# Attention loads in pairs of tokens and pairs of chunks, with a block swap on GpSimd and a new order of the output turn

## The chip, the cores and the metric

The kernel runs on one core of a Trainium2 chip. A core has five engines with their own instruction queues: TensorE (PE; its weight loads are listed as PEld), VectorE (DVE), ScalarE (ACT), GpSimd (POOL) and SyncE (SP). SP only issues DMAs here. Engines meet through semaphores, and each engine works its queue strictly in order. The metric is the device time of one execution in microseconds (us), lower is better.

## The reference

The program is causal windowed attention, then two mixtures of experts. Only the attention is touched by the change. Cut to what matters:

```
q, k, v: [4 batch, 8 heads, 576 tokens, 64]
scores = q @ k.T / 8 ; bias = -slope[h] * |i - j| ; kept where 0 <= i - j < 128
attn   = softmax(scores + bias)            # rows
x      = (attn @ v) -> [2304 tokens, 512]  # heads side by side
x      = soft MoE(x; phi, w1, w2)          # 8 experts, 4 slots each
out    = Sinkhorn-gated MoE(x; w_gate, m1, m2)
```

The array x is 2304 by 512, all inputs are float32, and the two expert stages read 33.5 MB of weights each.

## The kernel before

**Tiles and steps.** Two batch items go together (j = 0, 1), so there are two pairs of items, each with nine chunks of 64 query tokens: 18 tiles t. A step s is one tile and one half of the heads: t = s // 2, half hf = s % 2, so there are 36 steps. A half has four heads, in two head pairs g. A chunk sees its own and the two chunks before it: 192 keys.

**One step.** `emit_qk` (L169) makes scores in PSUM on TensorE. `emit_sm` (L188) adds the bias and takes the row extreme on VectorE, four operations at L203. `emit_exp` (L209) takes exponentials on ScalarE. One step later `emit_nm` (L216) scales the rows on VectorE by the reciprocal sums: L219, L220 and four operations at L222, which read and write SBUF alone. Two steps later `emit_pt` (L224) turns the weights on TensorE and ScalarE copies them out of PSUM (L234). Three steps later `emit_pv` (L237) multiplies by the values. After the second half of a tile, VectorE copies the outputs to `xT` (L271). `emit_x` (L273), called by `turned` (L464), turns them on TensorE and ScalarE copies them to `xn` (L278). After every fourth tile, `group` (L343) adds the logits of the first mixture (L284) and its running sums, in slices of one a step.

**Queries and keys.** `load_nat` (L127) loads one chunk of k and one of q, token per partition: 64 partitions for each batch item, eight heads of 64 numbers each, so a DRAM run is 256 bytes. `emit_tr` (L147) turns them on TensorE, and VectorE copies them to `kT`, a ring of four chunks, and to `qT`. For ring places that must be readable past the ring's end, ScalarE makes a second copy (L158). Keys are turned for the next tile in the first half's step, queries two head pairs a step, right after the scores.

**Orders and pools.** The order of the work is the order in which the step loop (L475 to L526) calls these functions: it fixes every engine's queue. PSUM has three banks for turns (`ps_t`, tag "pt", used in rotation by every turn and by the logits) and three for scores (`ps_s`). SP's queue carries all loads in program order: k and q, v (`load_v`), and the weights of the expert stages, prefetched one part a step by `load_part` (L57) from the list `pre` (L455).

**Heads of the second item.** The score multiply puts head a of item j into partitions by `a ^ j` (L182), so the second item's rows would come out with two heads exchanged: the bias table `rel_sb` has a second version for it (L440, L450), and `emit_pv` undoes it (L262).

Of the kernel before, what the change touches and what calls it, by code (L numbers as in the profile page):

```python
# [20 lines left out]
NPRE = 8  # L21
# [3 lines left out]
def tile_kernel(ctx: ExitStack, tc: tile.TileContext, q, k, v, phi, w1, w2, w_gate, m1, m2, rel, out):  # L25
# [69 lines left out]
    with tc.manual_schedule():  # L95
        with ExitStack() as ab:
# [5 lines left out]
            with ExitStack() as at:  # L102
                nat = at.enter_context(tc.tile_pool(name="nat", bufs=2))
# [14 lines left out]

                rel_sb = one.tile([128, 2, 4, 192], F32, name="rel_sb")


                qT = one.tile([128, 4, 2, 64], F32, name="qT")
# [4 lines left out]
                def load_nat(t):  # L127
                    bp, c = divmod(t, NCH)
                    for nm, src in (("k", k), ("q", q)):
                        nt_ = nat.tile([128, H, D], F32, tag=nm + "n", name=nm + "n")  # L130
                        for j in range(2):
                            nc.sync.dma_start(
                                out=nt_[CH * j:CH * j + CH],
                                in_=src[2 * bp + j, :, CH * c:CH * c + CH, :].rearrange("h i d -> i h d"))
                        natt[nm, t] = nt_
# [11 lines left out]
                def emit_tr(t, nm, gs=range(4)):  # L147
                    src = natt[nm, t]
                    ps = ps_t.tile([128, 4, 128], F32, tag="pt", name="pt")
                    for i, g in enumerate(gs):  # L150
                        nc.tensor.transpose(
                            ps[:, i, :], src[:, 2 * g:2 * g + 2, :].rearrange("p a d -> p (a d)"), idn)
                    pv_ = ps[:, 0:len(gs), :].rearrange("p g (j i) -> p g j i", j=2)
                    if nm == "k":
                        sl_ = t % 4
                        nc.vector.tensor_copy(out=kT[:, :, :, CH * sl_:CH * sl_ + CH], in_=pv_)
                        if sl_ < 2 and t >= 4:
                            nc.scalar.copy(out=kT[:, :, :, CH * (sl_ + 4):CH * (sl_ + 5)], in_=pv_)  # L158
                    else:
                        nc.vector.tensor_copy(out=qT[:, gs[0]:gs[-1] + 1], in_=pv_)  # L160
# [8 lines left out]
                def emit_qk(s):  # L169
# [3 lines left out]
                    k0 = CH * ((t - nch + 1) % 4)  # L173
# [4 lines left out]
                    for gg in range(2):  # L178
                        g = 2 * hf + gg
                        for j in range(2):  # L180
                            for a in range(2):
                                r0, c0 = CH * (a ^ j), CH * a  # L182
                                nc.tensor.matmul(ps[j][c0:c0 + CH, gg, col:192], lhsT=qT[r0:r0 + CH, g, j, :],
# [4 lines left out]
                def emit_sm(s):  # L188
# [8 lines left out]
                    for hh in range(4):  # L197
# [7 lines left out]
                            in1=rel_sb[:, j, 2 * hf + gg, col:192], scale=-0.125, scalar=3e38,  # L205
# [31 lines left out]
                def emit_pv(s):  # L237
# [18 lines left out]
                    for i0 in range(0, len(steps), 2):  # L256
                        for gg in range(2):
                            g = 2 * hf + gg
                            for i in (i0, i0 + 1):
                                j, vc, r0, r1, blk = steps[i]  # L260
                                for a in range(2):
                                    o = 128 * blk + 64 * (a ^ j)  # L262
# [116 lines left out]
                def group_end():  # L379
# [17 lines left out]
                    mm = sc_[:, 0, 0:NS]  # L397
# [10 lines left out]
                    selx = sc_[:, 0, NS:2 * NS]  # L408
                    selc = sc_[:, 0, 2 * NS:3 * NS]
# [6 lines left out]
                    rcs = sc_[:, 0, 3 * NS:4 * NS]  # L416
# [20 lines left out]
                load_nat(0)  # L437
                nc.sync.dma_start(out=rel_sb[:, 0, 3, :], in_=rel)
                for j in range(2):
                    nc.sync.dma_start(out=rel_sb[CH * j:CH * j + CH, 1, 3, :], in_=rel[CH * (1 - j):CH * (2 - j), :])  # L440
                load_nat(1)
# [3 lines left out]
                emit_tr(0, "k")  # L445
                warm(None, ps, idn, 3)
                for g in range(4):
                    eng = nc.scalar.mul if g < 2 else nc.gpsimd.tensor_scalar_mul
                    for j in range(2):
                        eng(rel_sb[:, j, g, :], rel_sb[:, j, 3, :], -(2.0 ** (2 - 2 * g)))  # L450
                emit_tr(0, "q", range(0, 2))
                emit_tr(0, "q", range(2, 4))

                NST = 2 * NT
# [791 lines left out]
```

## Time and profile before

| | us |
|---|---|
| median of 3 runs | 967.4 (966.14 to 967.91) |
| the profiled execution, its own time | 964.41 |
| span of the profile (first to last instruction) | 962.6 |
| TensorE busy in the span | 925.3 (96%) |
| VectorE busy | 739.3 (77%) |
| ScalarE busy | 611.4 (64%) |
| GpSimd busy | 542.1 (56%) |

The shares are averages over stages with different limits. The attention is the first 16% or so of the span; after that the expert stages keep TensorE nearly always busy. The attention's step loop runs from 8.0 us (first bias operation of step 0) to 142.1 us (first bias operation of step 35). A row of the profile that ends in brackets says how long the engine was idle just before it, and who ended the wait.

### The profile page before, as it was taken

How to read it: one execution, taken by the hardware profiler on the slowest of the kernel's cores; microseconds unless marked ns; L12 is line 12 of the kernel's file. 1: busy time of each engine (PE TensorE's matmuls, PEld its weight loads, DVE VectorE, ACT ScalarE, POOL GpSimd, SP SyncE). 2: the span in 40 equal slices, each digit the busy share in tenths (PEclk: the TensorE clock that was granted, in tenths of full speed). 3: DMA queues.
4: the chain of work that ended last, by engine and by line, in shares of the span. 5: the costliest groups of instructions: out<-in, count | busy, mean ns of one | idle time of the engine just before them, and what ended most of it. 6: DMA issues, size and time to landing. Idle time of an engine off the chain costs nothing.

```text
span 962.6 us, 24531 instructions
## 1 busy us (share of the span) xinstructions
PE 925.3 (96%) x9629; PEld 781.5 (81%) x9629; DVE 739.3 (77%) x1920; ACT 611.4 (64%) x1493; POOL 542.1 (56%) x624
## 2 busy tenths in 40 slices
PE   7898889889999999999999999999999999999997
PEld 5666665357888888888888888888888888888886
DVE  6988896666888777787778777877777778777775
ACT  5877784746777777666656664766576656764442
POOL 1000001214688579848974986589658956985442
PEclk9999999999999999999999999999999999999999
DMA  8999998960200400140023002200220020001222
GB/s 184 251 254 233 265 296 291 379 232 2 99 2 2 153 35 2 25 164 1 2 79 109 1 1 90 99 1 2 94 94 1 2 97 4 1 2 34 56 47 64
DMA packets 94659, 90.20 MB, mean 94 GB/s; under 512 B 63696, under 2 KB 67792, under 8 KB 94544
## 3 DMA queue, kind: packets, MB, share of 16 engines
q1 hardware_dynamic: 94544, 88.64, 32.1%
q8 instruction: 75, 1.23, 0.5%
q14 instruction: 40, 0.33, 0.1%
HBM read 82.07 MB, written 4.72 MB: 90 GB/s over the span
## 4 chain that ended last, share of the span: by engine, by line
PE 74%; DVE 2%; ACT 1%; issue 0%; DVEq 0%
PE x L1051 38%; PE y L1051 28%; PE z L979 6%; PE m L681 1%; DVE ops L992 0%; DVE s L1004 0%; PE m L556 0%; DVE acc L1063 0%; DVE prob L948 0%; ACT acc L1061 0%; ACT ops L989 0%; DVE rs L936 0%; ACT r L1000 0%; PE m L942 0%; ACT t L564 0%
## 5 line engine op out<-in xcount | busy, mean ns | idle before, releaser
L1051 PEld LDWEIGHTS <-ops 128*128 128x128 f16 x6048 | 591.9, 98 | 75.5 <-issue 4.9
L1011 POOL TENSOR_TENSOR ops<-s,ops 128x512 f16<-128x512 f32 x287 | 332.0, 1159 | 224.2 <-ACT ops L1008 218.2
L1051 PE MATMUL x<-w2h,ops 128*128 128x256 f16 x2304 | 414.3, 273 | 3.9 <-ACT acc L1061 2.7
L1051 PE MATMUL y<-w2h,ops 128*128 128x256 f16 x1728 | 318.3, 273 | 0.1
L1051 PE MATMUL x<-w2l,ops 128*128 128x256 f16 x1152 | 314.2, 273 | 0.0
L1008 ACT CAST ops<-s 128x512 f16<-128x512 f32 x288 | 177.6, 617 | 212.6 <-DVE s L1004 210.2
L1051 PE MATMUL y<-w2l,ops 128*128 128x256 f16 x864 | 235.1, 273 | 0.0
L1065 DVE SCALAR_TENSOR_TENSOR acc<-x,pe,acc 128x256 f32<-128x256 f32 x252 | 121.7, 483 | 77.3 <-PE x L1051 75.8
L989 ACT ACTIVATE ops<-z 128x512 f16<-128x512 f32 x216 | 128.4, 594 | 36.0 <-PE z L979 33.1
L992 DVE SCALAR_TENSOR_TENSOR ops<-z,ops 128x512 f16<-128x512 f32 x216 | 146.9, 680 | 0.0
L1065 DVE SCALAR_TENSOR_TENSOR acc<-y,pe,acc 128x256 f32<-128x256 f32 x189 | 91.3, 483 | 58.4 <-PE y L1051 58.0
L639 POOL TENSOR_TENSOR w2l<-w,w2h 128x256 f16<-128x256 f32 x168 | 112.3, 672 | 0.0
L1004 DVE SCALAR_TENSOR_TENSOR s<-z,r 128x512 f32<-128x512 f32 x144 | 98.2, 682 | 11.1 <-ACT r L1000 3.8
L1004 DVE SCALAR_TENSOR_TENSOR s<-z,s 128x512 f32<-128x512 f32 x144 | 98.1, 681 | 5.6 <-ACT ops L989 4.1
L979 PE MATMUL z<-ct,stk 128*128 128x256 f16 x576 | 86.3, 273 | 1.4 <-ACT stk L724 0.7
L774 POOL MEMSET hz<- 128x480 f32 x2 | 1.0, 498 | 141.0 <-ACT fo L313 139.7
L642 ACT CAST w2h<-w 128x256 f16<-128x256 f32 x168 | 67.4, 401 | 0.3 <-POOL w L639 0.3
L979 PEld LDWEIGHTS <-stk 128*128 128x128 f16 x576 | 55.7, 98 | 10.8 <-issue 2.6
L212 ACT ACTIVATE et<-et,mx 128x192 f32<-128x192 f32 (+2 forms) x144 | 61.3, 436 | 3.3 <-DVE mx L203 3.2
L1000 ACT ACTIVATE r<-z 128x512 f32<-128x512 f32 x72 | 42.4, 589 | 0.7 <-PE z L979 0.7
L639 POOL TENSOR_TENSOR w<-w 128x256 f32<-128x256 f32 x56 | 40.8, 729 | 0.0
L564 ACT ACTIVATE t<-w 128x512 f32<-128x512 f32 x64 | 40.2, 629 | 0.6 <-DMA w<-in_moe_w_dram 0.2
(192 smaller groups left out, 887.0 us busy)
## 6 DMA issues: line engine op xcount, KB each, us to landing
w<-in_moe_w_dram SPq DMA_DIRECT2D x68, 512.0 KB, 6.8
w<-in_moe_w_dram SPq DMA_DIRECT2D x14, 2048.0 KB, 8.2
kn<-in_k_dram SPq DMA_DIRECT2D x36, 128.0 KB, 5.5
qn<-in_q_dram SPq DMA_DIRECT2D x36, 128.0 KB, 5.5
v<-in_v_dram SPq DMA_DIRECT2D x18, 256.0 KB, 6.1
out_dram<-acc SPq DMA_DIRECT2D x34, 128.0 KB, 2.4
w<-in_moe_w_dram SPq DMA_DIRECT2D x2, 1024.0 KB, 7.8
stk<-sh SPq DMA_DIRECT2D x56, 16.0 KB, 1.8
```

The lines of the kernel that those rows point to most:

```text
L212: nc.scalar.activation(out=runs[hh], in_=runs[hh], func=AF.Exp, bias=mx[:, hh:hh + 1], scale=-1.0, accum_out=sm[:, hh:hh + 1])
L639: nc.gpsimd.tensor_tensor(out=out_, in0=x_, in1=y_, op=ALU.subtract)
L642: nc.scalar.copy(out=hi[:, i, r], in_=src[:, r])
L979: nc.tensor.matmul(ps[:, i], lhsT=stk[e][:, 128 * ft:128 * ft + 128], rhs=ct.rearrange("p (a n) t -> p a n t", a=2)[:, :, n, :], start=Tru ...
L989: nc.scalar.activation(out=ops_[m][:, k_, 0], in_=zb(m, i, j), func=AF.Relu)
L992: nc.vector.scalar_tensor_tensor(out=ops_[m][:, k_, 1], in0=zb(m, i, j), scalar=0.0, in1=ops_[m][:, k_, 0], op0=ALU.max, op1=ALU.subtract)
L1000: nc.scalar.activation(out=new_sum(m, "r21"), in_=zb(m, 2, 1), func=AF.Relu)
L1004: nc.vector.scalar_tensor_tensor(out=new_sum(m, nm), in0=zb(m, i, j), scalar=0.0, in1=o, op0=ALU.max, op1=op)
L1008: nc.scalar.copy(out=ops_[m][:, k_, 0], in_=sm_[m, nm])
L1011: eng.tensor_tensor(out=ops_[m][:, k_, 1], in0=sm_[m, nm], in1=ops_[m][:, k_, 0], op=ALU.subtract)
L1051: nc.tensor.matmul(out_, lhsT=a_[:, k_, l_, i, :], rhs=r_[:, k_, i, :], start=(first and j == 0), stop=(j == 11), skip_group_check=True)
L1065: nc.vector.scalar_tensor_tensor(out=o, in0=ps, scalar=pe_[e][:, t:t + 1], in1=o, op0=ALU.mult, op1=ALU.add)
```

## The change

Chunks are loaded in units of two (the ninth chunk of a pair of items alone), for one half of the heads: a tile `nt_` holds, in each partition, two neighbouring tokens of four heads. Each batch item has half of the partitions (64, or 32 in a single chunk's unit). A DRAM run is two tokens of one head, 512 bytes. The first item's half comes with one DMA, the second's with two, which put each head in the place of its neighbour. GpSimd then exchanges the two middle blocks of 64 numbers, with three copies through `swap`, so that the two heads of one token stand side by side. `emit_tr` turns four blocks into one bank, and one copy with a stride puts the tokens back in order, for two chunks at a time. The pool `nat` has four buffers for k and q together.

The second version of the bias table goes, with its two loads and the multiplies on GpSimd. Keys and queries of a unit are both turned in the two steps before its first tile, after the weights' turn of the step, and both copied then. `turned`, which turned the outputs right after the score multiply, now stands after the weights' turn, the exponentials and these turns, just ahead of the products with the values. Weights of the first mixture come in halves (1 MB) at odd steps, in place of quarters (512 KB) at every step. The loads of phi and the gate go to the start. In `group_end` four small values get tiles of their own. The core of the diff:

```
-                    bp, c = divmod(t, NCH)
-                    for nm, src in (("k", k), ("q", q)):
-                        nt_ = nat.tile([128, H, D], F32, tag=nm + "n", name=nm + "n")
-                        for j in range(2):
-                            nc.sync.dma_start(
-                                out=nt_[CH * j:CH * j + CH],
-                                in_=src[2 * bp + j, :, CH * c:CH * c + CH, :].rearrange("h i d -> i h d"))
+                units = [(bp, c, min(2, NCH - c)) for bp in range(2) for c in range(0, NCH, 2)]
+                wanted = [(u, nm, hf) for u in range(len(units)) for hf in range(2) for nm in "kq"]
+                def load_nat():
...
+                    nt_ = nat.tile([128, 2, 4, D], F32, tag="n", name=nm + "n")
+                    r1 = 32 * n
+                    for j in range(2):
+                        rows = nt_[r1 * j:r1 * j + r1].rearrange("p g (x r) d -> p g x (r d)", r=2)
+                        heads = src[2 * bp + j, 4 * hf:4 * hf + 4, CH * c:CH * (c + n), :].rearrange(
+                            "(g x) (p r) d -> p g x (r d)", x=2, r=2)
+                        if j == 0:
+                            nc.sync.dma_start(out=rows.rearrange("p g x e -> p (g x) e"),
+                                              in_=heads.rearrange("p g x e -> p (g x) e"))
+                        else:
+                            for x in range(2):
+                                nc.sync.dma_start(out=rows[:, :, 1 - x, :], in_=heads[:, :, x, :])
+                    all_ = nt_[0:2 * r1]
+                    nc.gpsimd.tensor_copy(out=swap[0:2 * r1], in_=all_[:, :, 1, :])
+                    nc.gpsimd.tensor_copy(out=all_[:, :, 1, :], in_=all_[:, :, 2, :])
+                    nc.gpsimd.tensor_copy(out=all_[:, :, 2, :], in_=swap[0:2 * r1])
...
+                    def place(x_, o):
+                        return x_[:, 2 * hf:2 * hf + 2, :, o:o + w].rearrange("q g j (p r) -> q r (g j) p", r=2)
                     if nm == "k":
+                        nc.vector.tensor_copy(out=place(kT, CH * (c % 4)), in_=pv_)
+                        if c and c % 4 == 0:
+                            nc.scalar.copy(out=place(kT, CH * 4), in_=pv_)
                     else:
+                        nc.vector.tensor_copy(out=place(qT, 0), in_=pv_)
...
-                    if 1 <= s and s - 1 < NST:
-                        t1, hf1 = divmod(s - 1, 2)
-                        if t1 + 1 < NT:
-                            emit_tr(t1 + 1, "q", range(2 * hf1, 2 * hf1 + 2))
-                    turned()
...
                         emit_exp(s)
-                        if t + 1 < NT and hf == 0:
-                            emit_tr(t + 1, "k")
+                        u = next((i for i, x_ in enumerate(units) if NCH * x_[0] + x_[1] == t + 1), None)
+                        if u is not None:
+                            emit_tr(u, "k", hf)
+                            emit_tr(u, "q", hf)
+                            for _ in range(2):
+                                load_nat()
+
+                    turned()
                     if 3 <= s and s - 3 < NST:
                         emit_pv(s - 3)
```

TensorE's queue of step 11 before (L183 scores, L151 turn of queries, L276 turn of the outputs `xT`, L233 turn of the weights `et`, L263 products with the values, L284 logits), up to the scores of step 12:

```order
L183 MATMUL s<-kT,qT 64x192 x8
L151 MATMUL pt<-idn,qn 128x128 x2
L276 MATMUL pt<-idn,xT 128x128 x4
L233 MATMUL pt<-idn,et 128x128 x6
L263 MATMUL xp<-ptt,v 64x64 x16
L284 MATMUL pt<-xT,phi_sb 32x128 x16
L183 MATMUL s<-kT,qT 64x192 x8
```

The same step now (L210 scores, L260 turn of the weights, L174 turns of keys and queries, L303 turn of the outputs, L290 products with the values, L311 logits):

```order
L210 MATMUL s<-kT,qT 64x192 x8
L260 MATMUL pt<-idn,et 128x128 x6
L174 MATMUL pt<-idn,kn 128x128 x4
L174 MATMUL pt<-idn,qn 128x128 x4
L303 MATMUL pt<-idn,xT 128x128 x4
L290 MATMUL xp<-ptt,v 64x64 x16
L311 MATMUL pt<-xT,phi_sb 32x128 x16
L210 MATMUL s<-kT,qT 64x192 x8
```

The output turn has moved behind the weights' turn, and a unit's keys and queries are turned between the two, so five turns and the logits take the three banks in that order.

VectorE's queue between the row scaling of step 10 and the bias of step 11 before (L222 scaling, L156 keys, L271 outputs, L160 queries, L203 bias):

```order
L222 TENSOR_SCALAR et<-et,rc 128x192 x4
L156 COPY kT<-pt 128x8x64
L271 COPY xT<-xp 128x4x64 x2
L160 COPY qT<-pt 128x256
L203 ISA et,mx<-s,rel_sb 128x192
```

The same place now (L249 scaling, L182 keys, L186 queries, L298 outputs, L230 bias):

```order
L249 TENSOR_SCALAR et<-et,rc 128x192 x4
L182 COPY kT<-pt 128x2x4x64
L186 COPY qT<-pt 128x2x256
L298 COPY xT<-xp 128x4x64 x2
L230 ISA et,mx<-s,rel_sb 128x192
```

The copy of the queries no longer stands straight ahead of the bias: both copies are twice as deep in tokens and come in two steps of four.

SP's queue at the start before, up to the fourth chunk's keys:

```order
L132 DMA kn<-in_k_dram 64x8x64 x2
L132 DMA qn<-in_q_dram 64x8x64 x2
L438 DMA rel_sb<-in_alibi_dram 128x192
L440 DMA rel_sb<-in_alibi_dram 64x192 x2
L132 DMA kn<-in_k_dram 64x8x64 x2
```

And now, up to the keys of the second unit:

```order
L146 DMA kn<-in_k_dram 64x4x128
L150 DMA kn<-in_k_dram 64x2x128 x2
L146 DMA qn<-in_q_dram 64x4x128
L150 DMA qn<-in_q_dram 64x2x128 x2
L466 DMA rel_sb<-in_alibi_dram 128x192
L146 DMA kn<-in_k_dram 64x4x128
L150 DMA kn<-in_k_dram 64x2x128 x2
L146 DMA qn<-in_q_dram 64x4x128
L150 DMA qn<-in_q_dram 64x2x128 x2
L469 DMA phi_sb<-in_moe_phi_dram 128x4x32
L470 DMA wg_sb<-in_moe_w_gate_dram 128x4x8
```

The first step's scores now stand behind thirteen DMAs (two chunks, both halves of the heads, and the bias), where they stood behind five.

## Rows read from the trace of the kernel before

**Rows 1.** The page's chain that ended last, shares of the span by line

```profile
PE x L1051 38%; PE y L1051 28%; PE z L979 6%; PE m L681 1%; DVE ops L992 0%; DVE s L1004 0%; PE m L556 0%; DVE acc L1063 0%; DVE prob L948 0%; ACT acc L1061 0%; ACT ops L989 0%; DVE rs L936 0%; ACT r L1000 0%; PE m L942 0%; ACT t L564 0%
```

**Rows 2.** Busy time by stretch: us, PE, PEld, DVE, ACT, POOL busy, clock, DMA, GB/s

```profile
19.56:142.07 122.51, 107.82 (x1851) 79.96 (x1849) 109.58 (x547) 93.37 (x347) 0.00 (x0) 0.99 1.08 257
```

**Rows 3.** Waits of VectorE, 8.0 to 142.1 us: total, times, longest

```profile
DVE qT L160 <- PE pt L151: 11.3, 11, 2.5
DVE kT L156 <- PE pt L151: 1.3, 1, 1.3
```

**Rows 4.** Timeline of VectorE in steps 8 and 9: start us, us, instruction

```profile
35.37 1.01 DVE L222 TENSOR_SCALAR et<-et,rc 128x192 f32<-128x192 f32 x4
36.29 0.68 DVE L156 COPY kT<-pt 128x512 f32<-128x512 f32 x1
36.90 0.75 DVE L271 COPY xT<-xp 128x256 f32<-128x256 f32 x2
37.56 0.42 DVE L160 COPY qT<-pt 128x256 f32<-128x256 f32 x1
37.89 0.35 DVE L203 CUSTOM_DVE_ANT_0 et<-s,rel_sb 128x192 f32<-128x192 f32 x1
...
39.41 1.01 DVE L222 TENSOR_SCALAR et<-et,rc 128x192 f32<-128x192 f32 x4
```

**Rows 5.** Waits of TensorE, 8.0 to 142.1 us

```profile
PE pt L276 <- DVE xT L271: 7.5, 8, 1.3
...
PE pt L151 <- DMA kn<-in_k_dram: 1.8, 2, 1.5
```

**Rows 6.** Timeline of TensorE in step 11

```profile
45.41 0.63 PE L276 MATMUL pt<-idn,xT 128*128 128x128 f32 x4 [0.65 <-DVE xT L271]
...
46.63 1.08 PE L263 MATMUL xp<-ptt,v 128*64 128x64 f32 x32
47.63 1.08 PE L284 MATMUL pt<-xT,phi_sb 128*32 128x128 f32 x32
48.65 0.88 PE L183 MATMUL s<-kT,qT 64*64 64x192 f32 x16
```

**Rows 7.** ScalarE by line, 19.5 to 142.1 us: busy us, mean ns, idle before

```profile
L158 ACT COPY kT<-pt 128x512 f32<-128x512 f32 x8 | 4.7, 585 | 4.5 <-DVE kT L156 4.5
```

**Rows 8.** Timeline of SP at the start

```profile
0.74 1.45 SPq L132 DMA_DIRECT2D kn<-in_k_dram  x2
...
5.43 1.30 SPq L132 DMA_DIRECT2D kn<-in_k_dram  x2
```

**Rows 9.** The page's DMA issues: count, KB each, us from issue to landing

```profile
stk<-sh SPq DMA_DIRECT2D x56, 16.0 KB, 1.8
```

**Rows 10.** Timeline of TensorE at the start

```profile
9.33 0.66 PE L151 MATMUL pt<-idn,kn 128*128 128x128 f32 x4 [1.45 <-DMA kn<-in_k_dram]
```

**Rows 11.** Timeline of VectorE at the start

```profile
8.03 0.22 DVE L203 CUSTOM_DVE_ANT_0 et<-s,rel_sb 128x64 f32<-128x64 f32 x1 [0.35 <-PE s L183]
```

**Rows 12.** GpSimd by line, 0 to 200 us: busy us, mean ns, idle before

```profile
L450 POOL TENSOR_SCALAR rel_sb<-rel_sb 128x192 f32<-128x192 f32 x4 | 2.7, 689 | 5.3 <-DMA rel_sb<-in_alibi_dram 5.1
...
L436 POOL MEMSET ones<- 128x128 f32 x1 | 0.2, 204 | 0.0
```

**Rows 13.** Timeline of VectorE, 182 to 193 us, in the first expert stage

```profile
182.47 2.69 DVE L598 SCALAR_TENSOR_TENSOR w2l<-w,w2i,w2h 128x256 f16<-128x256 f32 x4
...
191.48 1.66 DVE L598 SCALAR_TENSOR_TENSOR w2l<-w,w2i,w2h 128x256 f16<-128x256 f32 x4
```

**Rows 14.** Timeline of GpSimd in the same stretch

```profile
182.61 1.48 POOL L614 TENSOR_TENSOR w<-w 128x512 f32<-128x512 f32 x1
...
192.37 0.44 POOL L851 COPY hz<-hT 128x32 f32<-128x32 f32 x1 [1.75 <-PE s L858]
```

**Rows 15.** Busy time by stretch, columns as in rows 2

```profile
6.00:12.00 6.00, 3.16 (x49) 2.11 (x49) 3.25 (x18) 2.70 (x13) 2.87 (x5) 1.00 0.71 163
...
200.00:204.00 4.00, 2.48 (x26) 1.35 (x19) 1.81 (x8) 0.47 (x1) 0.00 (x0) 1.00 1.00 409
```

More of the change, by code (lines that the diff above doesn't have):

```diff
@@ L102, in tile_kernel @@
             with ExitStack() as at:
-                nat = at.enter_context(tc.tile_pool(name="nat", bufs=2))
+                nat = at.enter_context(tc.tile_pool(name="nat", bufs=4))
                 one = at.enter_context(tc.tile_pool(name="a1", bufs=1))
@@ new lines, in tile_kernel @@
+                wanted = [(u, nm, hf) for u in range(len(units)) for hf in range(2) for nm in "kq"]
+                def load_nat():
+                    if not wanted:
+                        return
+                    u, nm, hf = wanted.pop(0)
+                    bp, c, n = units[u]
+                    src = {"k": k, "q": q}[nm]
+                    nt_ = nat.tile([128, 2, 4, D], F32, tag="n", name=nm + "n")
[14 more added lines that the diff above has]
+                    nc.gpsimd.tensor_copy(out=all_[:, :, 2, :], in_=swap[0:2 * r1])
+                    natt[u, nm, hf] = nt_
@@ L145, in load_v, with emit_tr @@
                     vt[bp, c, j] = t
[L147 to L153, printed above, removed]
+                def emit_tr(u, nm, hf):
+                    bp, c, n = units[u]
+                    w = CH * n
+                    src = natt.pop((u, nm, hf))
+                    ps = ps_t.tile([128, 512], F32, tag="pt", name="pt")
+                    for i in range(4):
+                        r, g = divmod(i, 2)
+                        nc.tensor.transpose(ps[:, w * i:w * i + w],
+                                            src[0:w, g, 2 * r:2 * r + 2, :].rearrange("p x d -> p (x d)"), idn[0:w, 0:w])
+                    pv_ = ps[:, 0:4 * w].rearrange("q (r m p) -> q r m p", r=2, p=w // 2)
+                    def place(x_, o):
+                        return x_[:, 2 * hf:2 * hf + 2, :, o:o + w].rearrange("q g j (p r) -> q r (g j) p", r=2)
                     if nm == "k":
[L155 to L158, printed above, removed]
+                        nc.vector.tensor_copy(out=place(kT, CH * (c % 4)), in_=pv_)
+                        if c and c % 4 == 0:
+                            nc.scalar.copy(out=place(kT, CH * 4), in_=pv_)
                     else:
-                        nc.vector.tensor_copy(out=qT[:, gs[0]:gs[-1] + 1], in_=pv_)
+                        nc.vector.tensor_copy(out=place(qT, 0), in_=pv_)
                 sc = {}
@@ L396, in group_end @@
                     lg = sp.tile([128, 128], F32, tag="lt", name="lg", bufs=1)
-                    mm = sc_[:, 0, 0:NS]
+                    mm = sp.tile([128, NS], F32, name="mm", bufs=1)
                     m1_, fl = small("m1_"), small("fl")
@@ L436, in tile_kernel @@
                 nc.gpsimd.memset(ones, 1.0)
[L437 to L441, printed above, removed]
+                for _ in range(2):
+                    load_nat()
+                nc.sync.dma_start(out=rel_sb[:, 3, :], in_=rel)
+                for _ in range(2):
+                    load_nat()
+                nc.sync.dma_start(out=phi_sb, in_=phi.rearrange("(c p) s -> p c s", p=128))
+                nc.sync.dma_start(out=wg_sb, in_=w_gate.rearrange("(c p) s -> p c s", p=128))
                 ps = warm(ps_t, "pt", idn, 8)
@@ L477, in tile_kernel @@
                     if s < NST:
[L478 to L484 removed]
+                        if s > 2 and s % 2 and pre:
                             load_part(*pre.pop(0))
```

49 lines of the change are left out of this document (23 added, 26 removed).

## The prediction

> **What bounds the kernel now.** I read the chain of waits first [rows 1]: after the attention, TensorE's products at L1051 hold the end, and no idle time behind them is left to absorb anything. So I take every microsecond that the attention's loop gains or loses as one at the end. Then the busy time by stretch [rows 2]: in 122.51 us, 31 steps of 3.95 us, VectorE is busy 109.58 and TensorE 107.82. The DMA share is about 1, and yet the waits name few DMAs. VectorE is the busiest and its gaps set the pace. Its waits [rows 3]: 11.3 us in 11 gaps for `qT` and 1.3 for `kT`, both on TensorE's turns, 12.6 in all. In the timeline of VectorE [rows 4] the reader is to see a step without a gap: bias and row scaling 39.41 − 37.89 + (36.29 − 35.37) = 2.44 us, a 512-element copy 0.61 (start to next start), a pair of output copies 0.66, a 256-element copy 0.33. TensorE's waits [rows 5] show where its turns get late: 7.5 us in front of the output turn L276, on `xT`; for DMAs of `kn` only 1.8. The first of [rows 6] is such a wait. Between its start and the products, 45.41 to 46.63, stand ten blocks, four of the output turn and six of the weights' turn; so an output turn takes 0.49. Products take 1.00 and logits 1.02 to the next start, scores 0.88.
>
> **Part 1, the start.** The first scores stand behind 13 DMA issues instead of five. An issue takes SP 1.30 / 2 = 0.65 [rows 8], so the 13th starts at 0.74 + 12 × 0.65 = 8.5. The last is 32 KB; its landing lies between 1.8 us (16 KB, [rows 9]) and 3.25 (128 KB: issued at 5.43 + 0.65 = 6.08, turned at 9.33 [rows 8, 10]); I take 2.7, a little above the middle, since the others of the unit are still under way. Then three GpSimd copies of 128 elements. No row has one: a MEMSET of 128 takes 0.204, the TENSOR_SCALAR of 192 takes 0.689, or 0.46 by elements [rows 12]; I take 0.3, so 0.9 for three (0.6 to 1.4). A turn 0.5, a copy 0.6, first scores 0.2. Sum 13.4, where the first bias was at 8.03 [rows 11]: **+5.4** (by the ends of both, +4.2 to +6.5, and up to +7 if all loads of the first unit slow each other).
>
> **Part 2, fewer and longer copies.** Behind the first bias VectorE made 17 copies of 512 and 34 of 256: 17 × 0.61 + 34 × 0.33 = 21.6 us. Now 32 copies of 512 and 8 of 256 in all, four of the large ones before the first bias: 28 × 0.61 + 8 × 0.33 = 19.7. **−1.9**, if the strided write costs nothing; the copy of `kT`, which already writes in pieces of 64, is no slower per element than that of `qT`, so I keep 0. If it cost a tenth, +1.8 would come back.
>
> **Part 3, VectorE's gaps.** The output turn no longer holds up what VectorE waits for, since the weights' and queries' turns come before it. But a unit now makes TensorE take three banks for five turns (order of step 11 in the section on the change), and the bank of a unit's keys is wanted again by the third turn behind it. The copy of `kT` ends 2.44 + 0.68 = 3.12 us behind the step's bias, that of ScalarE in every fourth chunk 0.585 later [rows 7]. I go through the steps:
> - step 7, two output turns: the second one waits for the ring copy, 3.7, then 0.49 + 1.00 + 0.88 = 6.1 to the next scores, where VectorE is through at 2.44 + 2 × 0.61 = 3.66: a gap of 2.4;
> - step 11, logits: 3.12 + 1.02 + 0.88 = 5.0 against 3.66: 1.3; step 15 the like, with half a unit, 1.5;
> - step 16: the loads of the second pair's first unit are issued only two steps ahead. 6 issues × 0.65 + 3.2 + 0.9 = 8.0 against two steps of 3.95: with the turn, 1.2;
> - steps 19 and 27, logits without a unit: turn, products, logits and scores (0.49 + 1.00 + 1.02 + 0.88 = 3.4) follow the output copies, and VectorE has 1.5 and 2.4 of work beside them: 1.9 and 1.0;
> - steps 2 to 4 and 9: 0.5 and 0.1, by what VectorE waits there before, without the waits for the first unit's queries.
>
> Sum 9.9 in place of 12.6: **−2.7**. Bounds: 7 (steps 7, 11 and 15 lose half) and 12 left over, −5.6 to −0.6.
>
> **Part 4, GpSimd beside VectorE.** GpSimd did nothing in the loop [rows 2]; now it makes 3 × 40 = 120 copies, 24 of them for the first two units, so 96 in the loop. What they cost VectorE shows in the expert stage: four L598 take 2.69 with a GpSimd operation of 1.48 beside them and 1.66 with a copy of 0.44 beside them [rows 13, 14]. So a long one cost 1.03, and the short copy nothing that can be seen, but was itself slow. The scaling L222, which reads and writes SBUF, is the operation at risk: 0.92 of 3.95 us. A copy of 0.3 meets it with a chance of (0.92 + 0.3) / 3.95 = 0.31: 30 of 96. Between nothing and the whole 0.3 I take 0.07 each, nearer to the short row: **+2.1** (0 to +9).
>
> The Trainium skill ("SBUF — State Buffer", section "Who interferes with whom") says that VectorE in its two-port mode, which tensor_scalar can enter, and GpSimd share one pair of ports, and that whoever comes first holds it for the whole instruction while the other waits. By that rule part 4 would be up to +9; the slow 1.03 agrees, the 1.66 beside a short copy does not show it [rows 13].
>
> **Part 5, what I cost at nothing.** The DMA issues for q, k and these weights go from 104 to 136 on SP, which has time: 32 × 0.65 = 21 us over 140. Runs of 512 bytes move faster: the stretch 6 to 12 us gives 163 / 0.71 = 230 GB/s at full share with 256-byte runs, large rows 409 [rows 15]. The 72 loads of 128 KB are 9.4 MB, 41 us at 230 and 23 at 409: up to 18 us of DMA time. But only 1.8 us of waits are on `kn` [rows 5], which are in the sum of part 3. The multiplies on GpSimd for the second bias table were beside the start's loads and free nothing. Weights in halves: the same bytes in half the issues; no wait for them shows in the loop.
>
> **Sum.** +5.4 − 1.9 − 2.7 + 2.1 = +2.9. The profiled execution took 964.4, so 967.3; the median of the runs is 3.0 above that execution, 970.3 on the median.
>
> **Rivals.**
> - *The banks don't bind* (faster). Steps 7, 11, 15 and 16 hold 2.4 + 1.3 + 1.5 + 1.2 = 6.4 us of my gaps. If copies come earlier than I think, for instance because VectorE is behind TensorE there and has its scaling already done, they go: 970.3 − 6.4 = 963.9. For it: before, TensorE's longest waits were not on `kT` in front of a turn [rows 5]. Against it: there were four turns a step at most, and the keys' turn came later.
> - *The lock is dear* (slower still). 30 meetings × 0.3 = 9.0 in place of 2.1: 977.2. The point from which it decides is 0.2 us a meeting. For it the 1.03 us [rows 13]; against it the short copy. It is the skill's rule above.
> - *The loop hangs on the DMA queues* (much faster). Their share is 1.08 [rows 2]; if transfers paced it unseen, through v, k and q together, up to 18 us go: some 950 to 955. Against it: the waits of TensorE on keys' DMAs are 1.8 us in the loop [rows 5]. The Trainium skill ("DMA: Bandwidth & Descriptors", section "Specifications") wants transfers of at least 512 bytes for line rate; that the 256-byte runs go at 230 of 409 agrees.
> - *The start costs nothing*, because the loop catches up: the first steps have gaps of their own. Then 970.3 − 5.4 = 964.9, the same place as the first rival, with which it shares its chance.
>
> **How the numbers follow.** A difference under 0.2%, 1.9 us either way, cannot be told from no change: 965.5 to 969.3. Forecast, 967 to 973: 0.47, of which 0.19 fall within 0.2% and 0.28 are slower. Faster by the banks or the start: 0.30, of which 0.22 beyond 0.2% and 0.08 within. DMA paced: 0.04, faster. Lock dear: 0.15, slower. The rest, 0.04, lies within. Together faster 0.26, same 0.31, slower 0.43. Range 962.5 to 977.5: below it fall the DMA rival and the last of the banks' rival, above it the dearest locks.
>
> **What would show it.** First bias at 13.4 us; before, 8.03. Copies of queries and keys 28 and 8 in the loop with 0.6 and 0.33. Gaps of VectorE in steps 7, 11 and 15 with the scores as releaser, and behind them a TensorE turn or the logits that waited for `kT` or ScalarE's ring copy; in step 16 a turn that waited for GpSimd. The scaling L249 longer than 1.01 for four where a GpSimd copy lies beside. The forecast is wrong if the first bias comes before 12.2, if the sum of VectorE's gaps is under 7, or if four scalings take over 1.2 on the mean. If waits on `v` or weights had hidden behind SP's queue, the attention would end over 10 us earlier.

## The result, and the profile of the changed kernel

The change makes the kernel slower: 972.84 us median of 6 runs (970.69 to 974.18) against 965.88 (964.74 to 967.91); the ratio is 1.0069, with a 95% interval of 1.0053 to 1.0084. The forecast was 970.3, in a range of 962.5 to 977.5. The profiled execution took 972.96 with a span of 971.2, where before it was 964.41 and 962.6: 8.6 us more in the span. The difference of the medians is 7.0.

Busy time by stretch of the changed kernel, columns as in [rows 2] (us, then busy us of TensorE, its loads, VectorE, ScalarE and GpSimd, granted clock, DMA share, GB/s): the loop from the first bias operation to step 35's, and four stretches that begin in it or just ahead of it:

```profile
13.80:152.09 138.29, 121.84 (x1964) 89.89 (x1965) 118.64 (x587) 98.92 (x382) 32.62 (x109) 0.93 0.90 239
9.70:19.90 10.20, 8.73 (x82) 6.17 (x82) 6.84 (x40) 4.82 (x26) 3.84 (x14) 0.50 0.47 119
23.40:30.20 6.80, 6.53 (x80) 4.63 (x82) 4.59 (x27) 3.39 (x13) 1.76 (x6) 0.50 0.88 205
64.30:67.70 3.40, 3.36 (x28) 2.33 (x28) 1.30 (x9) 0.06 (x1) 1.72 (x6) 0.51 0.10 39
84.80:88.20 3.40, 3.40 (x40) 2.88 (x44) 1.13 (x2) 0.59 (x1) 2.04 (x7) 0.50 0.76 200
```

The loop begins 5.8 us later (13.80 against 8.03, [rows 11]) and takes 138.3 us, where it took 134.0 (8.03 to 142.07): its last step begins 10.0 us later. A clock of 0.50 is 1.2 GHz, where 1.00 is 2.4; the four stretches have it, 23.8 us in all, of which 4.1 lie ahead of the first bias. The same view of the kernel before shows two such stretches in the loop, 6.8 us:

```profile
12.00:15.40 3.40, 3.26 (x24) 2.21 (x22) 2.74 (x23) 2.56 (x13) 0.00 (x0) 0.50 1.13 211
87.10:90.50 3.40, 3.40 (x29) 2.42 (x26) 2.67 (x16) 1.85 (x9) 0.00 (x0) 0.50 0.95 177
```

Behind the loop the span gets 1.4 us back (10.0 at the loop's end, 8.6 in the span); no run tests why.

Where VectorE waits, in its timeline in the changed kernel (in brackets the idle time ahead of the instruction):

```profile
13.80 0.23 DVE L230 CUSTOM_DVE_ANT_0 et<-s,rel_sb 128x64 f32<-128x64 f32 x1
...
25.68 0.36 DVE L230 CUSTOM_DVE_ANT_0 et<-s,rel_sb 128x192 f32<-128x192 f32 x1 [2.08 <-PE s L210]
...
42.13 0.36 DVE L230 CUSTOM_DVE_ANT_0 et<-s,rel_sb 128x192 f32<-128x192 f32 x1 [2.46 <-PE s L210]
...
57.52 0.36 DVE L230 CUSTOM_DVE_ANT_0 et<-s,rel_sb 128x192 f32<-128x192 f32 x1 [1.38 <-PE s L210]
...
65.27 0.29 DVE L386 COPY lg<-pt 128x128 f32<-128x128 f32 x1 [1.20 <-PE pt L345]
...
66.75 0.36 DVE L230 CUSTOM_DVE_ANT_0 et<-s,rel_sb 128x192 f32<-128x192 f32 x1 [1.13 <-PE s L210]
...
77.36 0.36 DVE L230 CUSTOM_DVE_ANT_0 et<-s,rel_sb 128x192 f32<-128x192 f32 x1 [1.67 <-PE s L210]
...
85.92 0.69 DVE L186 COPY qT<-pt 128x512 f32<-128x512 f32 x1 [0.69 <-PE pt L174]
...
88.67 0.23 DVE L230 CUSTOM_DVE_ANT_0 et<-s,rel_sb 128x64 f32<-128x64 f32 x1 [2.06 <-PE s L210]
...
94.76 0.29 DVE L230 CUSTOM_DVE_ANT_0 et<-s,rel_sb 128x128 f32<-128x128 f32 x1 [1.78 <-PE s L210]
...
125.20 0.36 DVE L230 CUSTOM_DVE_ANT_0 et<-s,rel_sb 128x192 f32<-128x192 f32 x1 [1.20 <-PE s L210]
```

The waits [rows 3] for `qT` in 11 places have become waits for scores in these, and one each in the middle of a step. The view of waits gives their sum from the first bias on:

```profile
DVE et L230 <- PE s L210: 14.1, 10, 2.5
DVE lg L386 <- PE pt L345: 1.2, 1, 1.2
DVE qT L186 <- PE pt L174: 0.7, 1, 0.7
DVE et L230 <- ACT et L239: 0.5, 1, 0.5
```

That is 16.5 us in place of 12.6. TensorE's timeline shows what lies ahead of the scores in steps 3, 7, 13 and 17:

```profile
21.01 0.63 PE L174 MATMUL pt<-idn,kn 128*128 128x128 f32 x4
21.76 0.86 PE L174 MATMUL pt<-idn,qn 128*128 128x128 f32 x4
22.98 0.33 PE L290 MATMUL xp<-ptt,v 64*64 64x64 f32 x4 [0.36 <-DMA v<-in_v_dram]
23.67 0.58 PE L290 MATMUL xp<-ptt,v 64*64 64x64 f32 x10 [0.36 <-DMA v<-in_v_dram]
...
24.15 1.49 PE L210 MATMUL s<-kT,qT 64*64 64x192 f32 x14
...
37.83 0.79 PE L174 MATMUL pt<-idn,qn 128*128 128x128 f32 x4 [1.06 <-POOL qn L153]
38.46 0.60 PE L303 MATMUL pt<-idn,xT 128*128 128x128 f32 x4
39.77 0.66 PE L303 MATMUL pt<-idn,xT 128*128 128x128 f32 x4 [0.71 <-ACT kT L184]
...
64.34 0.49 PE L290 MATMUL xp<-ptt,v 64*64 64x64 f32 x6 [2.18 <-issue]
...
83.71 0.79 PE L174 MATMUL pt<-idn,kn 128*128 128x128 f32 x4 [2.15 <-POOL kn L153]
```

Step 7 is the forecast's wait for ScalarE's ring copy, which ends after the wait for a load (1.06 us) ahead of it. In step 3 all is late in a row: the queries of the second unit's second half, the values behind them in SP's queue, and then scores at the half clock (1.49 us, 0.88 in [rows 6]). Those queries and values stand at the end of this stretch of SP's timeline, in which a tile takes three issues where two did [rows 8]:

```profile
8.08 1.26 SPq L150 DMA_DIRECT2D qn<-in_q_dram  x2
...
10.66 0.60 SPq L146 DMA_DIRECT2D kn<-in_k_dram  x1
...
17.34 1.82 SPq L150 DMA_DIRECT2D qn<-in_q_dram  x2
19.21 1.23 SPq L164 DMA_DIRECT2D v<-in_v_dram  x2
```

SP issues without a pause from 0.7 to 20 us. GpSimd's copies of that last tile end at 22.1. The wait in step 13 ("issue") has no cause in the profile, and no other run has a gap there.

### The profile page after: what moved, and what is told of

Read it like the earlier page. It is cut to its first block, busy times and chain, and to the rows that moved or that the text cites. A ratio compares the mean times of both kernels' runs of the same rounds, so it can differ in the third digit from the quotient of the medians.

```text
span 971.2 us, 24864 instructions
## 1 busy us (share of the span) xinstructions
PE 932.1 (96%) x9645; PEld 786.4 (81%) x9645; DVE 739.8 (76%) x1906; ACT 610.4 (63%) x1493; POOL 575.2 (59%) x740
## 4 chain that ended last, share of the span: by engine, by line
PE 73%; DVE 2%; ACT 0%; issue 0%; DVEq 0%
PE x L1076 37%; PE y L1076 28%; PE z L1004 6%; PE m L706 1%; DVE ops L1017 0%; DVE s L1029 0%; PE m L581 0%; DVE acc L1088 0%; DVE prob L963 0%; DVE rs L961 0%; DVE prob L973 0%; ACT ops L1014 0%; ACT r L1025 0%; ACT acc L1086 0%; PE m L967 0%
## 5 line engine op out<-in xcount | busy, mean ns | idle before, releaser
L152 POOL COPY swap<-kn 128x128 f32<-128x128 f32 (+1 forms) x20 | 6.2, 309 | 90.8 <-DMA kn<-in_k_dram 90.7
L230 DVE CUSTOM_DVE_ANT_0 et<-s,rel_sb 128x192 f32<-128x192 f32 (+2 forms) x144 | 39.4, 329 | 14.8 <-PE s L210 14.1
L261 ACT COPY ptt<-pt 128x384 f32<-128x384 f32 (+2 forms) x72 | 29.2, 444 | 24.7 <-PE pt L260 24.5
```

## The experiments

All are against the kernel before on the same chip; a ratio stands with its 95% interval, and the changed kernel's own, 1.0069 [1.0053, 1.0084], is what they are held against. A gap that is given for a step is the sum of VectorE's waits from that step's first bias to the next one's, in the run's profiled execution; it is also called the gap ahead of the next step. Two theories at first. A: the late first bias is carried to the end, with the gaps of banks. B: SP's issues pace the first steps, and some later ones, so the first bias does not matter by itself.

**Second half of the first unit turned behind step 0.**

The first lines stood ahead of step 0, the new ones stand behind `emit_exp`; two loads move along.

```
-                for nm in "kq":
-                    emit_tr(0, nm, 1)
...
+                        if s == 0:
+                            for nm in "kq":
+                                emit_tr(0, nm, 1)
...
```

> The changed kernel with one edit: keys and queries of the first unit's second half of the heads are turned behind step 0's exponentials, not ahead of its scores, and the two loads behind them move along. Theory A (the late start, +5.8 us at the first bias, is carried to the end): first bias near 9.4 us in place of 13.8 and the end 3 to 4.4 us earlier, near 969. Rival B (SP's issues pace the first steps: the eight loads of the first two units are 24 DMAs of 0.65 us, and step 3's turn needs the last of them, 22 us): first bias near 9.4 as well, but step 4 starts where it did, within 1 us of 25.7, and the time stays within 1 us of 972.8.

971.97 us, ratio 1.0063 [1.0039, 1.0087]: no difference that can be told from the changed kernel. VectorE's timeline, first bias of steps 0 and 1:

```profile
9.81 0.23 DVE L230 CUSTOM_DVE_ANT_0 et<-s,rel_sb 128x64 f32<-128x64 f32 x1 [0.67 <-PE s L210]
...
14.95 0.23 DVE L230 CUSTOM_DVE_ANT_0 et<-s,rel_sb 128x64 f32<-128x64 f32 x1 [0.91 <-PE s L210]
```

Step 0 begins 4 us earlier and step 1 where it did (14.97); step 4 begins at 26.2 (25.7). A falls as it was worded: the lateness of the first bias by itself is not carried. But step 1 still waits for the same 13 DMAs (two waits for turns of the first unit's second half, 0.50 and 1.68 us, stand ahead of its bias), so this run does not free the loop of the start. B stands.

**The first unit's loads of the second item from ScalarE's queue.**

```
+                    second = nc.scalar if len(wanted) >= 36 else nc.sync
-                                nc.sync.dma_start(out=rows[:, :, 1 - x, :], in_=heads[:, :, x, :])
+                                second.dma_start(out=rows[:, :, 1 - x, :], in_=heads[:, :, x, :])
```

> The changed kernel with one edit: for the first unit's four tiles the second item's two DMAs are issued by ScalarE's queue in place of SP's, so SP issues 5 DMAs ahead of the second unit in place of 13. Both A and B expect a gain here: first bias near 10, the second unit's loads some 5 us earlier, step 4 near 21, time 968 to 969. If neither the start nor SP's issues matter (the loop catches up later at waits of its own), the time stays within 1 us of 972.8. The two together (this run and e1) part A from B: A expects about the same gain in both, B a gain only here.

968.55 us, ratio 1.0025 [1.0012, 1.0039], 4.2 us better than the change (0.44% of 966). The first bias comes at 11.3 only (near 10 was expected), yet step 4 begins 2.8 us earlier, at 22.9 (near 21 was expected). A gain here and none above is what B expects. Eight issues fewer on one queue were worth over half of the loss.

**One DMA for the second item in all 40 tiles.**

```
...
-                            for x in range(2):
-                                nc.sync.dma_start(out=rows[:, :, 1 - x, :], in_=heads[:, :, x, :])
+                        nc.sync.dma_start(out=rows.rearrange("p g x e -> p (g x) e"),
+                                          in_=heads.rearrange("p g x e -> p (g x) e"))
```

> The changed kernel with the second item's two DMAs for each tile made one, which leaves its heads unexchanged (its pairs of heads come out exchanged and with each other's bias, so the output is not the reference's; all else is the same work). 80 DMAs for queries and keys in place of 120. Theory B (SP's issues pace the first steps): first bias at 13.8 - 4 x 0.65 = 11.2, the second unit's last copy at 22.1 - 8 x 0.65 = 17, gap ahead of step 4 under 0.7, time -4 to -6, 967 to 969. Rival (DMA bytes or landing pace it): first bias earlier by at most 1, time within 1.5 us of 972.8.

966.98 us, ratio 1.0009 [0.9996, 1.0023]: 5.8 us of the 6.7 are gone. The first bias comes at 11.63. VectorE's waits from there on, in this kernel:

```profile
DVE et L226 <- PE s L206: 9.9, 8, 2.2
DVE qT L182 <- PE pt L170: 0.2, 1, 0.2
```

and TensorE's step 3:

```profile
18.92 0.63 PE L170 MATMUL pt<-idn,kn 128*128 128x128 f32 x4
19.44 0.63 PE L170 MATMUL pt<-idn,qn 128*128 128x128 f32 x4
20.00 0.46 PE L286 MATMUL xp<-ptt,v 64*64 64x64 f32 x16
20.28 0.83 PE L206 MATMUL s<-kT,qT 64*64 64x192 f32 x16
```

Keys, queries, values and scores stand without a wait, at the full clock, where the changed kernel waits twice for values and multiplies at half the clock. The gaps of steps 3, 13 and 17 are gone or under 0.2; those of steps 7, 11, 15, 19 and 27, the forecast's, are there. Only step 3's can be put down to the issues: it is 1.2 to 3.2 us in the eight kernels with three issues a tile, and 0, 0, 0 and 1.4 in the four with two. Step 13's is in the changed kernel alone. Step 17's is missing in four kernels with three issues (the first experiment's, and those without the swap, with more warming and with quarters), and it is 3.4 us in one with two (the last below), so what makes it stays open.

**The same with the right heads.** The second item's four heads come in reverse order by one DMA, and its scores read the other head pair:

```
+                            nc.sync.dma_start(out=rows.rearrange("p g x e -> p (g x) e"),
+                                              in_=heads.rearrange("p g x e -> p (g x) e")[:, ::-1, :])
-    lhsT=qT[r0:r0 + CH, g, j, q0:q0 + CH], rhs=kT[r0:r0 + CH, g, j, k0:k1]
+    lhsT=qT[r0:r0 + CH, g ^ j, j, q0:q0 + CH], rhs=kT[r0:r0 + CH, g ^ j, j, k0:k1]
```

> The changed kernel with the second item's load as one DMA that takes the four heads in reverse order, and the score multiply reading the other head pair for that item: what the two DMAs gave, with 80 DMAs for queries and keys in place of 120. Theory B: as the run with one DMA for both items, first bias near 11.6, gap ahead of step 4 under 0.7, time near 967, within 0.2% of the kernel before. Rival (a reversed order of heads makes the transfer slower): landing later than 5 us at the start, time above 969.

970.38 us, ratio 1.0040 [1.0025, 1.0054]: better than the change, but by the ratios 3.0 us short of the run above. The first half of the loop is alike (first bias 11.81, step 4 at 21.0, step 16 at 69.4 against 70.4), and the keys' median landing is 3.8 us against 5.5. So the time is above 969, as the rival had it, but not by a slower transfer. In the profile the difference comes later: a stretch of 6.8 us at the half clock from 89 us, one behind the loop that is 3.4 us longer, and this in TensorE's timeline in step 28:

```profile
117.72 0.54 PE L210 MATMUL s<-kT,qT 64*64 64x192 f32 x4 [1.95 <-issue]
```

TensorE stops in the middle of a step's score multiplies, waiting for nothing that the profile shows, as it did in step 13 of the changed kernel (2.18 us). What stops it stays open, and so do the 3.0 us between two kernels that do the same work: the profile is that of the fastest execution here, 967.86, and the seven have a median granted clock of 0.986, where the twelve of the run above have 0.9915. Fewer issues are thus worth between 2.8 and 5.8 us.

**No block swap on GpSimd.**

```
-                    nc.gpsimd.tensor_copy(out=swap[0:2 * r1], in_=all_[:, :, 1, :])
-                    nc.gpsimd.tensor_copy(out=all_[:, :, 1, :], in_=all_[:, :, 2, :])
-                    nc.gpsimd.tensor_copy(out=all_[:, :, 2, :], in_=swap[0:2 * r1])
```

> The changed kernel without GpSimd's three copies for each tile: the two middle blocks of 64 numbers stay exchanged, so heads and tokens are mixed up and the output is not the reference's; all other work is the same. Prediction's terms: first bias 1.0 us earlier, near 12.8; scaling L249 back to 1.01 us for four from 328 to 316 ns a mean (-1.6 us); gap of step 17 smaller by about 1. Sum -2.5 to -4, so 969 to 970. Rival, dear lock: -7 us or more, 966 or below. Rival, copies hidden: within 1 us of 972.8.

969.55 us, ratio 1.0033 [1.0020, 1.0047], 3.5 us better. The row scaling by line (busy us, mean ns), in this kernel:

```profile
L246 DVE TENSOR_SCALAR et<-et,rc 128x192 f32<-128x192 f32 x104 | 26.2, 316 | 0.9
```

In the changed kernel, with its two copies of 512 elements:

```profile
L249 DVE TENSOR_SCALAR et<-et,rc 128x192 f32<-128x192 f32 x104 | 27.6, 328 | 0.9
...
L182 DVE COPY kT<-pt 128x512 f32<-128x512 f32 x14 | 9.5, 681 | 0.1
L186 DVE COPY qT<-pt 128x512 f32<-128x512 f32 x14 | 9.5, 679 | 0.7 <-PE pt L174 0.7
```

And in the kernel before:

```profile
L222 DVE TENSOR_SCALAR et<-et,rc 128x192 f32<-128x192 f32 x104 | 26.2, 316 | 0.9
```

GpSimd's copies cost the scaling 1.4 us in all, and with them gone it is exactly as before. The first bias is 0.8 us earlier. What makes the rest of the 3.5 is not shown: step 17's gap is gone, but steps 3, 7 and 15 have longer ones, and the sum is 15.7 us in place of 16.5. The dear lock (7 us or more) falls. The 1.4 us are five whole copies of 0.29 out of 108 in the loop, so what the meetings cost is far from 30 whole ones. The Trainium skill ("SBUF — State Buffer", section "Who interferes with whom") says that between VectorE in a two-port mode and GpSimd the one who comes second waits for the other's whole instruction. That the scaling took 328 ns with GpSimd's copies in the loop and 316 without them agrees; how often the two met, no run shows.

**More warming products at the start.**

```
                 emit_tr(0, "q", 0)
+                warm(None, ps, idn, 3)
...
+                emit_tr(0, "k", 1)
+                warm(ps_t, "pt", idn, 3)
+                emit_tr(0, "q", 1)
```

> The changed kernel with two groups of three more warming products on TensorE, between the turns of the first unit's halves, where it waits for loads (1.2 and 1.0 us idle). Theory C (the half clock from 9.6 to 19.5 and 23 to 30 us, which the trace of the changed kernel shows, is what makes the gap of 2.1 us ahead of step 4): the granted clock stays 1.0 over at least a part of these stretches, that gap falls under 0.7, and the time falls by 1 to 2.5 us. Rival: the clock stays up but the gap is that of loads (the turns of step 3 wait for GpSimd's copies of the last tile), and the time stays within 0.7 us.

971.84 us, ratio 1.0051 [1.0029, 1.0073]: not to be told from the change. In the profiled execution, the slowest of the seven (974.27) and the one with the lowest mean clock (0.984, the others 0.990 to 0.994), three stretches, columns as above:

```profile
8.00:19.00 11.00, 7.83 (x97) 5.33 (x95) 7.15 (x41) 5.89 (x31) 3.56 (x12) 1.00 0.44 112
20.30:27.10 6.80, 5.54 (x48) 3.52 (x52) 3.61 (x17) 1.50 (x7) 2.11 (x8) 0.50 0.70 164
37.40:44.20 6.80, 5.44 (x52) 4.45 (x56) 2.37 (x6) 2.58 (x7) 2.42 (x8) 0.50 0.76 179
```

And TensorE in step 7 of this kernel:

```profile
38.69 1.11 PE L174 MATMUL pt<-idn,kn 128*128 128x128 f32 x4 [2.78 <-POOL kn L153]
```

The clock holds through the start, and then falls when the next wait for loads comes, at 20.3 and at 37.4. The gap ahead of step 4 stays (3.1 us). In this execution the half clock follows waits; how much it costs by itself, this run does not settle.

**The output turn put back,** and in the kernel before its new place alone (the same edit with the signs turned):

```
                         emit_qk(s)
+                    turned()
+                    if s < NST:
                         emit_sm(s)
...
-                    turned()
                     if 3 <= s and s - 3 < NST:
                         emit_pv(s - 3)
```

> The changed kernel with the output turn put back where it stood: right behind the score multiply, ahead of the weights' turn. Theory of banks (the turn stands behind the unit's keys and queries and waits there for the copies of kT): the gaps ahead of steps 8, 12 and 16 (2.46, 1.38, 1.67 us) shrink to under 1 each, but TensorE waits again for the output copies in front of the turn (7.5 us in the kernel before), and the weights' turns come later; sum -1 to -3 us. Rival (the new place is the part that gains): +1 to +4 us.

> The kernel before with one part of the change alone: the output turn moved behind the weights' turn, the exponentials and the keys' turn, just ahead of the products with the values. From the kernel before: VectorE waited 11.3 us in 11 gaps for the queries' turns, of which 7.5 us are TensorE's waits in front of the output turn. If the output turn was what held them up, those gaps fall to 4 to 6 and the time is 3 to 6 us shorter, 960 to 963. Rival (the turn then waits for the bank of the keys' copy, as in the changed kernel): gaps move to the scores, and the time is within 1.5 us of 966.

The first took 975.19 us, ratio 1.0094 [1.0076, 1.0112], where 1 to 3 us less were expected; the gaps ahead of steps 8 and 16 are 1.47 and 0, down as the theory of banks has it, but step 12's is 1.78 and new ones come, 1.99 ahead of step 26 among them. The second took 965.78, ratio 0.9990 [0.9975, 1.0005], its gaps 13.9 in place of 12.6; the 3 to 6 us that were expected did not come. By itself the move is worth nothing that can be measured; beside the units' turns it may be worth 2 us, but the intervals overlap.

**The first output turn put off by two steps, not three.**

```
-                            px.append((s + 3 * (t3 % 4 == 0), t3))
+                            px.append((s + 2 * (t3 % 4 == 0), t3))
```

> The changed kernel with one edit: the first of each four output turns is put off by two steps in place of three, so that steps 7, 15, 23 and 31 have one output turn each and steps 6, 14, 22 and 30 have the other. Theory of banks (the second output turn of step 7 waits for ScalarE's ring copy, whose bank it takes): the gaps ahead of steps 8 and 16 fall from 2.46 and 1.67 to under 0.7 each, nothing comes in steps 6 and 14 beyond 0.5, and the time falls by 2 to 3.5 us, to about 970. Rival (these gaps are of loads and the half clock, which follow the start): they stay within 0.7 and the time within 1 us of 972.8.

971.91 us, ratio 1.0057 [1.0041, 1.0073], not to be told from the change. Step 15's gap goes, as expected. Step 7's is 5.24 us: TensorE waits there for the loads, 2.48 us ahead of its turn of the keys at 38.76, and then multiplies at the half clock. This is the slowest of twelve executions (974.83, the fastest 966.53), so the gap need not be in all of them.

**Weights in quarters again.**

```
-                        if s > 2 and s % 2 and pre:
+                        if s > 1 and pre:
-                pre = [("w1", e, ..., p, 2) for e in range(NPRE) for p in range(2)]
+                pre = [("w1", e, ..., p, 4) for e in range(NPRE) for p in range(4)]
```

> The changed kernel with the weights of the first mixture in quarters at every step again (16 DMAs more on SP, all from step 2 on). The prediction costed the halves at nothing: time within 1 us of 972.8, first steps as they are. Theory B (SP's issues): +0.65 us of issue a step, of which the loads for step 17 are behind a few; +0.5 to +2 us. If the 1 MB transfers hold up the loads behind them, -1 to -3 us.

972.39 us, ratio 1.0054 [1.0041, 1.0068]: the halves are worth nothing that can be measured, as forecast. Nor do the 16 more issues, all behind step 2, cost the 0.5 to 2 us that B gave them. The profile also parts the waits from the clock in step 3, which here has the full clock:

```profile
21.67 0.86 PE L174 MATMUL pt<-idn,qn 128*128 128x128 f32 x4 [0.81 <-POOL qn L153]
22.93 0.84 PE L290 MATMUL xp<-ptt,v 64*64 64x64 f32 x14 [0.40 <-DMA v<-in_v_dram]
...
23.66 0.82 PE L210 MATMUL s<-kT,qT 64*64 64x192 f32 x14
```

The gap of step 3 is 1.20 us, as much as these two waits; in the changed kernel, with the scores at 1.49, it is 2.08.

**The mended kernel.** The reversed load with the first unit's second item from ScalarE's queue, and then the two-step delay on top:

```
+                            second.dma_start(out=rows.rearrange("p g x e -> p (g x) e"),
+                                             in_=heads.rearrange("p g x e -> p (g x) e")[:, ::-1, :])
...
+                            px.append((s + 2 * (t3 % 4 == 0), t3))
```

> The same, and the first unit's loads of the second item issued by ScalarE's queue: 5 issues on SP ahead of the second unit. Theory B: first bias near 9.5, further 1.5 to 2.5 us, time 964.5 to 965.5, at or just under the kernel before. Rival (then the banks and the half clock set the first eight steps): within 0.7 us of the run with the reversed load alone.

> The same again, with the first of each four output turns put off by two steps in place of three. Theory of banks: gaps ahead of steps 8 and 16 (2.35 and 2.07 us in the run with one DMA) go, and with the clock at full in step 7 the time falls by 2 to 4 us more, to 961 to 963, clear of the kernel before. Rival (the gap of step 7 is no matter of that turn): the gap ahead of step 8 stays over 2, that of step 16 goes, time -1 to -2.

967.06 us, ratio 1.0005 [0.9993, 1.0017], and 965.97, ratio 0.9993 [0.9981, 1.0006]. The first is 3.3 us better than the reversed load alone, but not for the reason expected (first bias near 9.5). A GpSimd and a VectorE row of it:

```profile
9.14 0.30 POOL L153 COPY swap<-kn 128x128 f32<-128x128 f32 x1 [1.37 <-DMA kn<-in_k_dram]
...
12.82 0.23 DVE L231 CUSTOM_DVE_ANT_0 et<-s,rel_sb 128x64 f32<-128x64 f32 x1
```

These keys were issued at 2.15 us by ScalarE and at 3.09 by SP, and came 6 us after the later of the two; in the reversed load alone they were there at 7.9 and the first bias at 11.81. The loads issued in the first 8 us have median landings of 3.9 to 5.5 us here, 2.5 to 2.8 in the changed kernel. So with the issues out of the way it is the landing of the loads that holds the start. Step 16 begins 2 us later than in the reversed load alone (71.4 against 69.4); what is gained lies behind step 20, where that run had gaps of 1.06 and 1.84 us.

In the second, VectorE's row ahead of step 8 reads

```profile
37.88 0.36 DVE L231 CUSTOM_DVE_ANT_0 et<-s,rel_sb 128x192 f32<-128x192 f32 x1 [0.51 <-PE s L211]
```

where the first has 3.22 us and the reversed load alone 2.46; step 16's gap is 0, with 1.57 and 1.56 in those two. So the two output turns in one step do cost what the forecast said. But step 3 has a gap of 1.4 us again and step 17 one of 3.4 in this profile, beside stretches at the half clock (10.1 to 23.8 and 75.0 to 81.8), and the time fell by 1.1 us only, with intervals that overlap, where 2 to 4 were expected. Neither version beats the kernel before.

## Why the prediction was right, and where it was not

The direction, the range and the mechanism by which the first bias comes late were right; the size was less than half (+2.9 forecast, 8.6 in the profiled span, 7.0 in the medians). That 970.3 lies only 2.5 us under the median measured is luck in part: it was added to a median of three runs, 967.4, where six give 965.88. The parts as measured, 5.8 − 1.9 + 3.9 + 1.4 = 9.2, make up most of the 10.0 by which the loop's last step is later.

- *Part 1, the start, +5.4.* Measured 5.8. The 13th issue ends at 9.3, the copies take 0.29 each (0.3 taken), the first bias comes at 13.80 (13.4). The last load is 64 KB, not 32 as the forecast says, but loads of this size took the 2.7 us that it gave them (queries in the first 8 us). What the term was taken to mean was wrong: with the first bias 4 us earlier the time did not change, because step 1 waited for the same unit and step 4 for the next. Nor do the issues alone make the start: with five on SP and four on ScalarE's queue ahead of it, it came at 12.8.
- *Part 2, copies, −1.9.* Right by counts and durations: 28 and 8 from the first bias on, at 0.68 and 0.42 us. The strided write costs nothing.
- *Part 3, gaps, −2.7.* This is the step that failed: +3.9 (12.6 to 16.5). Forecast and measured, step by step: 7, 2.4 and 2.46; 11, 1.3 and 1.38; 15, 1.5 and 1.67; 19, 1.9 and 1.78; 27, 1.0 and 1.20. The reading of the banks from the order and a few durations held to a tenth or two in this profile; at the half clock it does not (step 15 has 3.0 us in four other kernels, with a stretch of it there). Missed were step 3 (0.5 for steps 2 to 4, measured 2.2), step 13 (nothing, 2.3) and the loads of the second pair (1.2 in step 16, measured 2.8 in step 17). The first was taken "by what VectorE waits there before". It should have been counted on from part 1: by 0.65 us an issue, the 14 behind the 13th end at 0.74 + 27 × 0.65 = 18.3 (measured 19.2), they land and are swapped after 21, and step 3 wants the last. Of its 2.1 us ahead of step 4 some 1.2 are such waits and the rest goes with the half clock, by the run with quarters. The gaps of steps 13 and 17 come and go between kernels with the same loads; their cause stays open. With 40 issues fewer, the sum of the gaps was 10.1, near the forecast's 9.9.
- *Part 4, GpSimd, +2.1.* 1.4 for the scaling of 192 columns. The row of the short copy was the right neighbour, and the whole lock was not.
- *Part 5.* "SP has time", 21 us over 140, was an average, and wrong in the first 20 us, in which SP is never idle. The loop's DMA share fell (1.08 in [rows 2], 0.90 now), and no run shows time gained by it. Halves of weights at nothing: right.
- *The rivals.* The banks do bind. The lock is cheap. The loop does hang on the queues in its first steps, but by the number of issues and so the other way. An earlier first bias alone was worth nothing because something else was as late, not because the loop catches up.

The clock was in none of the terms. It was at its lower level for 19.7 us of the loop in place of 6.8, and the stretches that the rows show begin in or soon after waits of TensorE. What part of the gaps of steps 13 and 17 it makes was not parted from the waits themselves. For the whole, an estimate: in 201 executions on record, each compared with others of its kernel, 0.01 less of mean granted clock goes with 3.2 us more; the medians are 0.987 for the changed kernel and 0.993 for the one before, so some 2 of the 7.0 us go with the clock, whether as cause or as a companion of late loads.

## What to carry to other kernels

Where a load is split into more DMAs, count the issuing queue's work up to each deadline, not over the whole stage: at 0.65 us each, 27 issues set when step 3 could have its queries. Count the landing as well: with the issues out of the way, loads took up to 6 us to come, and the start was only 1 us earlier. A late first result says little by itself; ask for what the next steps wait. An order of turns over a few banks, worked through by hand with measured durations, came out to a tenth or two of a microsecond where the inputs were in time and the clock was full. And compare the profiles of several kernels before a gap is given a cause: two of the three that the forecast missed were not in every kernel with the same loads.

## What the runs showed of the hardware

- Most of SP's issues of queries and keys took the same time for 64 KB as for 128 KB, 0.60 to 0.65 us; one pair in the first 20 us took 1.82.
- Queries and keys issued in the first 8 us landed 2.5 to 2.8 us later in the median in the changed kernel, and 3.9 to 5.5 us later in the run with the reversed load on two queues.
- The granted clock went to 0.50 at 37.4 us in the run with more warming products, within a wait of 2.78 us of TensorE, and at 64.3 and 84.8 us in the changed kernel, at the end of a wait of 2.18 and 1.1 us after one of 2.15. The stretches in the rows lasted 3.4 to 10.2 us.
- TensorE stood still for 2.18 us in the changed kernel and for 1.95 us in the run with the reversed load, between multiplies of one group, with nothing in the profile to wait for.
